# One shared rotation of five PSUM banks in place of three plus two, and 36 stores moved to another engine's DMA queue

## Chip, cores and metric

The kernel runs on one core of a Trainium2 chip. The metric is the device time of one execution in microseconds (us). Most executions of one kernel agree within about 0.4%.

Ratios in this text are the mean time of one kernel's fast runs over that of the other's from the same rounds, with a 95% interval. They are therefore not exactly the ratio of the medians that stand beside them.

Short names: TensorE is PE, VectorE is DVE, ScalarE is ACT, GpSimd is POOL, SyncE is SP in profile lines.

## The reference

The kernel computes the forward pass and all gradients of one layer that adds three terms: the input, a gated feed-forward part ("FFN"), and a state-space convolution ("S4").

```python
xn  = layernorm(x)                                   # 2048 x 576, bf16
gate, up = xn @ W_gate, xn @ W_up                    # 2048 x 4608
ffn = ((gate * (gate > 0)) * up) @ W_down
dt  = exp(log_dt); logdA = dt * (A_re + 1j*A_im)     # 576 x 128
K   = einsum("dn,dnl,dn->dl", C, exp(logdA * l), dt*B).real
out = x + irfft(rfft(xn) * rfft(K)) + xn*Dskip + ffn
# the outputs: out and the gradients of x, A, B, C, log_dt, Dskip, W_gate, W_up, W_down
```

## The kernel before

The FFN part is matmul-bound. It goes through F = 4608 in 12 chunks of 384, and each chunk through the 2048 rows in four groups. The S4 part is a second program, a Python generator, whose instructions are interleaved with FFN's in time. The framework that builds the kernel may order the instructions of each engine anew from their dependencies, so a change of pools or queues can change the instruction order as well.

Each matmul result lies in a PSUM bank until ScalarE or VectorE has copied it out. There are three pools of such banks:

```python
g.psum_mm = pool("psum_mm", 3, space=PSUM)   # FFN matmuls
g.psum_s4 = pool("psum_s4", 3, space=PSUM)   # everything of S4
g.psum_t  = pool("psum_t",  2, space=PSUM)   # FFN transposes
```

The parts of FFN that the argument touches (cuts are marked):

```python
def a_unit(self, c, sg, ft, turns=()):               # first layer: gate, up, dh
    for i, rhs in enumerate((xT, xT, gT)):
        ps = g.psum_mm.tile([P, 512], F32, name="ps_mm")
        for k in range(NK):                           # L235: 5 matmuls of 512 columns
            nc.tensor.matmul(ps[:], lhsT=w[:, k, fs], rhs=rhs[:, k, :], ...)
        ...                                           # one transposition group between two of them
    nc.scalar.activation(rg[:], ps_g[:], ACT.Relu)                     # frees the bank of gate
    nc.vector.scalar_tensor_tensor(upm[:], rg[:], 0.0, ps_u[:], ...)   # frees the bank of up
    nc.vector.tensor_tensor(hT[:], rg[:], upm[:], op=ALU.mult)
    ...                                               # dhb copy frees the third; dgT, duT

def t_steps(self, units):                             # L264: transposes of hT, dgT, duT
    pt = g.psum_t.tile([P, 8, P], BF16, name="pt")
    ...
    g.bal.copy(dst[...], pt[:, 0:JS, :], 512, fp32=False)

def outdx(self, c, sg, j, ...):                       # L291: four output tiles of 288 columns
    ps = g.psum_mm.tile([P, 512], F32, name="ps_mm")
    ...                                               # 3 or 6 matmuls from hT, dgT, duT
    g.bal.copy(o[:, which, hs], ps[:, :DH], DH)       # the osx copy, mostly on ScalarE
```

The part of S4 whose stores move: 36 tiles of exponentials of 128x640 floats (320 KB) are made by VectorE and ScalarE, stored to memory, and read back much later.

```python
exp_ = self.pool(c, "par_ex", 5)                      # five exs buffers
def ex_step(i):
    ex = exp_.tile(shp, F32, name="exs")
    v.tensor_tensor(ex[:], pw[...], self.ev[...], op=ALU.mult)     # L568, VectorE
    nc.scalar.activation(ex[:], ex[:], ACT.Exp)                    # L569, ScalarE
    nc.sync.dma_start(self.ex_dram[:, i], ex[:])                   # L570
```

Of the kernel before, what the change touches and what calls it, by code (L numbers as in the profile page):

```python
# [9 lines left out]
BF16 = mybir.dt.bfloat16  # L10
F32 = mybir.dt.float32
# [3 lines left out]
P = 128  # L15
MAGIC = 12582912.0
TWO_PI = 2.0 * math.pi
PSUM = bass.MemoryType.PSUM
# [52 lines left out]
def dchunks():  # L71
    return [(k, k * P, min(P, D - k * P)) for k in range(NK)]
# [42 lines left out]
def ln_group(g, pools, sg, x4, gT):  # L115
    nc, bal = g.nc, g.bal
    sb, small = pools
    t0 = sg * JS
    mv = small.tile([P, JS, nc.vector.BN_AGGR_DIM], F32, name="mv")
    for j in range(JS):  # L120
        stats = small.tile([P, 2, nc.vector.BN_STATS_DIM], F32, name="stats")
        for s in range(2):
            nc.vector.bn_stats(out=stats[:, s, :], in_=x4[:, j, s * DH:(s + 1) * DH])
        nc.vector.bn_aggr(out=mv[:, j, :], in_=stats[:])
    mvb = small.tile([P, JS, 2], BF16, name="mvb")
    nc.vector.tensor_copy(mvb[:], mv[:])
    veb = small.tile([P, JS], BF16, name="veb")
    nc.vector.tensor_scalar(veb[:], mvb[:, :, 1], 1e-5, None, op0=ALU.add)
    sdb = small.tile([P, JS], BF16, name="sdb")
    nc.scalar.activation(sdb[:], veb[:], ACT.Sqrt)  # L130
    neg = small.tile([P, JS], F32, name="neg")
    nc.vector.tensor_scalar(neg[:], mvb[:, :, 0], -1.0, None, op0=ALU.mult)
    sdf = small.tile([P, JS], F32, name="sdf")
    nc.vector.tensor_copy(sdf[:], sdb[:])
    nc.vector.reciprocal(g.rinv[:, t0:t0 + JS], sdf[:])
    xn4 = sb.tile([P, JS, DP], BF16, name="xn4")
    nc.gpsimd.memset(xn4[:, :, D:DP], 0.0)
    xT = g.xtp.tile([P, NK, JS * P], BF16, name="xT")
    for j in range(JS):
        if j % 2 == 0:  # L140
            nc.vector.tensor_scalar(x4[:, j, :], x4[:, j, :], neg[:, j:j + 1], None, op0=ALU.add)
        else:
            nc.scalar.activation(x4[:, j, :], x4[:, j, :], ACT.Identity, bias=neg[:, j:j + 1])
    for j in range(JS):
        nc.vector.tensor_scalar(xn4[:, j, 0:D], x4[:, j, :], g.rinv[:, t0 + j:t0 + j + 1], None, op0=ALU.mult)
        pt = g.psum_t.tile([P, 8, P], BF16, name="pt")
        for k in range(NK):
            nc.tensor.transpose(out=pt[:, k, :], in_=xn4[:, j, k * P:(k + 1) * P], identity=g.ident_bf[:])
        (nc.vector.tensor_copy if j % 2 == 0 else nc.scalar.copy)(xT[:, :, j * P:(j + 1) * P], pt[:, 0:NK, :])  # L149
    nc.sync.dma_start(g.xT_dram[sg], xT[:])  # L150
    nc.sync.dma_start(g.xn_dram[:, t0:t0 + JS, :], xn4[:, :, 0:D])
    for k, d0, dsz in dchunks():
        nc.sync.dma_start(g.xs_dram[k][:, t0:t0 + JS, :], xn4[:, :, d0:d0 + dsz])
    bal.add(d=6.5, a=2.5)
    return xT, gT

class Ffn:
# [100 lines left out]
    def t_steps(self, units):  # L258
        g, nc = self.g, self.g.nc
        for c, sg, ft in units:  # L260
            for src, dst in zip(self.T[(c, sg, ft)], (self.hN, self.dgN, self.duN)):
                pt = g.psum_t.tile([P, 8, P], BF16, name="pt")
                for j in range(JS):
                    nc.tensor.transpose(out=pt[:, j, :], in_=src[:, j * P:(j + 1) * P], identity=g.ident_bf[:])  # L264
                g.bal.copy(dst[:, sg * JS:(sg + 1) * JS, ft * P:(ft + 1) * P], pt[:, 0:JS, :], 512, fp32=False)
                yield
# [194 lines left out]
class S4:  # L461
# [14 lines left out]
    def pool(self, ctx, name, bufs, side="left"):  # L476
        return ctx.enter_context(self.g.tc.tile_pool(name=name, bufs=bufs, side=side, reuse_waits="tile"))
# [68 lines left out]
    def params(self, pw):  # L546
        g, nc, bal = self.g, self.g.nc, self.g.bal
        v = nc.vector
        with ExitStack() as c:
            pool = self.pool(c, "par_raw", 1)  # L550
            exp_ = self.pool(c, "par_ex", 5)
            raw = pool.tile([P, 6, D], BF16, name="raw")
            nc.sync.dma_start(raw[:], self.par_in[:])
            ldt = pool.tile([P, D], BF16, name="ldt")
            nc.sync.dma_start(ldt[:], self.log_dt.rearrange("(o d) -> o d", o=1).to_broadcast([P, D]))
            yield 1.0
            dt = pool.tile([P, D], F32, name="dtf")
            nc.scalar.activation(dt[:], ldt[:], ACT.Exp)
            nc.sync.dma_start(self.dt_dram[:], dt[:])
            Ar, Ai, Br, Bi, Cr, Ci = (raw[:, i, :] for i in range(6))  # L560
            v.tensor_tensor(pw[:, 0, :], Ar, dt[:], op=ALU.mult)
            bal.add(d=0.7, a=0.7)
            yield 1.0

            def ex_step(i):
                shp = [P, SX, NE]
                ex = exp_.tile(shp, F32, name="exs")
                v.tensor_tensor(ex[:], pw[:, 0, i * SX:(i + 1) * SX].unsqueeze(2).to_broadcast(shp), self.ev[:].unsqueeze(1).to_broadcast(shp), op=ALU.mult)  # L568
                nc.scalar.activation(ex[:], ex[:], ACT.Exp)  # L569
                nc.sync.dma_start(self.ex_dram[:, i], ex[:])  # L570
                bal.add(d=0.75, a=0.65)

            for i in range(0, 8):
                ex_step(i)
                yield 1.0
            p1 = pool.tile([P, D], F32, name="p1")
            p2 = pool.tile([P, D], F32, name="p2")
            v.scalar_tensor_tensor(pw[:, 1, :], Ai, 1.0 / TWO_PI, dt[:], op0=ALU.mult, op1=ALU.mult)
            for j, (y1, y2, op) in enumerate(((Br, Bi, ALU.subtract), (Bi, Br, ALU.add))):
                v.tensor_tensor(p1[:], Cr, y1, op=ALU.mult)  # L580
                v.tensor_tensor(p2[:], Ci, y2, op=ALU.mult)
                v.tensor_tensor(p1[:], p1[:], p2[:], op=op)
                v.tensor_tensor(pw[:, 2 + j, :], p1[:], dt[:], op=ALU.mult)
                bal.add(d=2.6)
                yield 2.0
            for i in range(8, D // SX):
                ex_step(i)
                yield 1.0
# [489 lines left out]
def kernel(  # L1078
# [25 lines left out]
    nc = tc.nc  # L1104
    rows = lambda ap: ap.flatten_outer_dims().rearrange("(p t) d -> p t d", p=P)
    g = G()
# [2 lines left out]
    g.out_dskip = out_9  # L1109
    pool = lambda name, bufs, **kw: ctx.enter_context(tc.tile_pool(name=name, bufs=bufs, **kw))  # L1110
    g.consts = pool("consts", 1)
    g.psum_mm = pool("psum_mm", 3, space=PSUM)
    g.psum_s4 = pool("psum_s4", 3, space=PSUM)
    g.psum_t = pool("psum_t", 2, space=PSUM)
    g.dram = pool("dram", 1, space=DRAM)
    make_consts(g)
    d = lambda name, shape, dt=BF16: g.dram.tile(shape, dt, name=name)
# [14 lines left out]
    def ln(sg, *args):  # L1132
        r = ln_group(g, ln_pools, sg, *args)
        done[0] += 1
        if done[0] == NSG:
            lnctx.close()
        return r
# [79 lines left out]
```

## Time and profile before

| | before |
|---|---|
| median time | 1816.37 us (6 runs, 1814.77 to 1818.72) |
| TensorE busy | 96% |
| VectorE, ScalarE busy | 75%, 65% |
| sum of TensorE's idle gaps | 72.7 us |

The page of the kernel before, its first two parts and lines of its fifth and sixth. The last line, of the sixth part, ends with the median time from issuing a transfer to the signal that it is complete; this text calls that landing. A group's line gives the instruction, its count, its busy time and mean duration, and after the second bar the idle time of its engine just before it and what ended most of it:

```profile
PE 1736.5 (96%) x16449; PEld 1185.3 (65%) x16449; DVE 1359.2 (75%) x3181; ACT 1185.5 (65%) x2710; POOL 205.4 (11%) x246
...
DMA  8788999678568566776857856856665577994873
...
L67 ACT CAST osx<-ps_mm 128x288 bf16<-128x288 f32 x675 | 261.9, 426 | 70.3 <-PE ps_mm L291 67.1
...
L291 PE MATMUL ps_mm<-wf,dgT 128*128 128x288 bf16 x1152 | 207.3, 287 | 12.8 <-ACT osx L67 6.5
...
ex_dram<-exs SPq DMA_DIRECT2D x36, 320.0 KB, 3.8
```

TensorE is the limit. The second group waits before it starts, and what it waits for is the osx copy. That copy only reads a bank; the matmuls do not read its result. So this is a wait for a free bank. The waits of TensorE in the kernel before (us in total, times, longest):

```profile
PE ps_mm L204 <- DMA gT<-in_gT_dram: 8.9, 1, 8.9
PE ps_mm L291 <- DVE upm L245: 8.1, 12, 1.1
PE ps_mm L291 <- ACT osx L67: 6.5, 10, 1.8
PE ps_mm L235 <- ACT obd L67: 4.7, 2, 4.5
...
PE ps_mm L291 <- DVE hT L247: 3.8, 3, 1.9
PE ps_mm L291 <- ACT dhb L67: 3.5, 8, 1.0
```

Matmuls overlap, so short waits vanish inside "busy". A finer count takes the interval between successive matmul starts, less the usual interval after a matmul of that shape, and books the excess on whatever released the later matmul.

For the stores, the timeline of the kernel before from 121 to 147 us, with cuts (start, duration, engine, line, what; in brackets the idle time before and its releaser):

```profile
121.38 0.82 ACT L569 ACTIVATE exs<-exs 128x640 f32<-128x640 f32 x1
...
137.66 1.84 SPq L570 DMA_DIRECT2D ex_dram<-exs  x1
...
144.02 0.83 DVE L568 TENSOR_TENSOR exs<-pw,ev 128x640 f32<-128x640 f32 x1 [7.24 <-DMA ex_dram<-exs]
...
144.88 0.74 ACT L569 ACTIVATE exs<-exs 128x640 f32<-128x640 f32 x1 [7.74 <-DVE exs L568]
...
145.53 0.50 ACT L67 CAST obd<-ps_mm 128x432 bf16<-128x432 f32 x1
...
146.08 1.44 PE L235 MATMUL ps_mm<-gT,wd_160 128*128 128x512 bf16 x3 [4.46 <-ACT obd L67]
```

SyncE issued a store at 137.66 whose exponential was finished before. VectorE stood still 7.24 us for a buffer of exponentials, ScalarE 7.74 us behind it, and TensorE 4.46 us for the obd copy that stands behind the next exponential on ScalarE.

### The profile page before, as it was taken

What the parts mean: (1) busy time and instruction counts of PE and PEld (TensorE: products, weight loads), DVE (VectorE), ACT (ScalarE), POOL (GpSimd) and SP (SyncE); (2) the same over time, 40 slices, a digit from 0 to 9 for tenths busy, and PEclk for the clock granted to TensorE, in tenths of its full rate; (3) what the DMA queues carried; (4) which work ended last, traced back from release to release, by engine and by line L of the source; (5) the groups of instructions that cost most, each with busy time, mean ns of one, the idle gap of its engine ahead of it and who ended that gap; (6) DMA issues with size and microseconds to landing.
All of it is one profiled execution on the core that took longest, in us unless ns stands there. A gap on an engine that the chain in (4) does not pass through costs nothing. (4 is left out here: it accounts for less than half of the span.)

```text
span 1813.8 us, 42303 instructions
## 1 busy us (share of the span) xinstructions
PE 1736.5 (96%) x16449; PEld 1185.3 (65%) x16449; DVE 1359.2 (75%) x3181; ACT 1185.5 (65%) x2710; POOL 205.4 (11%) x246
## 2 busy tenths in 40 slices
PE   7998998999999999999999999999999999999998
PEld 5664556667566666766756766766676675676776
DVE  7575886676888789678787899989979863983551
ACT  5874874686578487568468658748746845764551
POOL 0200012012022011011102101101111100110000
PEclk9999999999999999999999999999999999999999
DMA  8788999678568566776857856856665577994873
GB/s 292 262 309 309 319 257 286 192 185 244 163 134 207 176 178 148 222 187 146 224 156 187 226 164 145 219 173 151 167 179 146 91 220 244 269 292 153 268 245 96
DMA packets 239004, 373.30 MB, mean 206 GB/s; under 512 B 49490, under 2 KB 153428, under 8 KB 237268
## 3 DMA queue, kind: packets, MB, share of 16 engines
q1 hardware_dynamic: 212836, 304.09, 51.4%
q0 software_dynamic: 24384, 51.92, 18.3%
q10 hardware_dynamic: 1584, 14.60, 2.3%
q8 instruction: 128, 2.10, 0.5%
q14 instruction: 72, 0.59, 0.1%
HBM read 233.10 MB, written 137.43 MB: 204 GB/s over the span
## 5 line engine op out<-in xcount | busy, mean ns | idle before, releaser
L67 ACT CAST osx<-ps_mm 128x288 bf16<-128x288 f32 x675 | 261.9, 426 | 70.3 <-PE ps_mm L291 67.1
L304 POOL DMA_DIRECT2D acc_dram<-osx x160 | 138.8, 868 | 1066.9 <-ACT osx L67 716.3
L291 PE MATMUL ps_mm<-wf,dgT 128*128 128x288 bf16 x1152 | 207.3, 287 | 12.8 <-ACT osx L67 6.5
L344 PEld LDWEIGHTS <-rows 128*128 128x128 bf16 x1536 | 146.2, 98 | 96.6 <-issue 6.9
L291 PE MATMUL ps_mm<-wf,duT 128*128 128x288 bf16 x1152 | 206.0, 287 | 0.0
L291 PE MATMUL ps_mm<-wf,hT 128*128 128x288 bf16 x1152 | 185.5, 288 | 13.4 <-DVE upm L245 6.8
L235 PE MATMUL ps_mm<-gT,wd_160 128*128 128x512 bf16 x705 | 178.0, 381 | 5.9 <-ACT obd L67 4.7
L235 PE MATMUL ps_mm<-xT,wd_158 128*128 128x512 bf16 x720 | 181.0, 379 | 0.8 <-ACT xT L149 0.5
L235 PE MATMUL ps_mm<-xT,wd_159 128*128 128x512 bf16 x720 | 179.9, 379 | 0.0
L245 DVE SCALAR_TENSOR_TENSOR upm<-rg,ps_mm 128x512 bf16<-128x512 bf16 x144 | 98.2, 682 | 92.2 <-PE ps_mm L235 70.4
L328 PE MATMUL ps_mm<-rows,hN 128*128 128x144 bf16 x2304 | 158.4, 226 | 0.0
L328 PEld LDWEIGHTS <-hN 128*128 128x128 bf16 x2304 | 147.4, 98 | 4.1 <-issue 1.4
L67 ACT CAST obw<-ps_mm 128x384 bf16<-128x384 f32 x104 | 49.6, 478 | 147.7 <-PE ps_mm L344 116.4
L344 PE MATMUL ps_mm<-dgN,rows 128*128 128x384 bf16 x768 | 137.7, 329 | 0.6 <-ACT rg L243 0.6
L291 PEld LDWEIGHTS <-dgT 128*128 128x128 bf16 x1152 | 107.3, 98 | 45.9 <-issue 20.7
L344 PE MATMUL ps_mm<-duN,rows 128*128 128x384 bf16 x768 | 136.6, 326 | 0.3 <-DVE upm L245 0.3
L291 PEld LDWEIGHTS <-hT 128*128 128x128 bf16 x1152 | 105.0, 98 | 43.2 <-issue 13.7
L291 PEld LDWEIGHTS <-duT 128*128 128x128 bf16 x1152 | 112.8, 98 | 29.2
L243 ACT ACTIVATE rg<-ps_mm 128x512 bf16<-128x512 f32 x144 | 87.1, 605 | 54.5 <-PE ps_mm L235 53.0
L903 DVE TENSOR_REDUCE Sm<-pr 128x8 f32<-128x256 f32 x288 | 118.9, 413 | 3.6
L67 ACT CAST dhb<-ps_mm 128x512 bf16<-128x512 f32 x141 | 83.9, 595 | 56.6 <-PE ps_mm L235 54.5
L235 PEld LDWEIGHTS <-wd_159 128*128 128x128 bf16 x720 | 65.3, 98 | 61.8 <-issue 1.5
(2517 smaller groups left out, 3523.5 us busy)
## 6 DMA issues: line engine op xcount, KB each, us to landing
acc_dram<-osx POOLq DMA_DIRECT2D x176, 288.0 KB, 4.7
gT<-in_gT_dram SPq DMA_DIRECT2D x48, 640.0 KB, 6.1
xT<-xT_dram SPq DMA_DIRECT2D x44, 640.0 KB, 5.7
rows<-in_gq_dram SPq DMA_DIRECT2D x48, 576.0 KB, 4.3
wf<-in_Wf_dram ACTq DMA_DIRECT2D x11, 1296.0 KB, 9.2
ex_dram<-exs SPq DMA_DIRECT2D x36, 320.0 KB, 3.8
ex<-ex_dram SPq DMA_DIRECT2D x36, 320.0 KB, 4.0
out_dram<-obw SPq DMA_DIRECT2D x96, 96.0 KB, 2.5
```

Source lines behind the costliest of these rows:

```text
L67: self.nc.scalar.copy(out, in_)
L235: nc.tensor.matmul(ps[:], lhsT=w[:, k, fs], rhs=rhs[:, k, :], start=(k == 0), stop=(k == NK - 1))
L243: nc.scalar.activation(rg[:], ps_g[:], ACT.Relu)
L245: nc.vector.scalar_tensor_tensor(upm[:], rg[:], 0.0, ps_u[:], op0=ALU.is_gt, op1=ALU.mult)
L291: nc.tensor.matmul(ps[:, cs], lhsT=lt, rhs=rh, start=(i == 0), stop=(i == len(mms) - 1))
L304: nc.gpsimd.dma_start(g.acc_dram[:, t, :, :], o[:], accum_op=ALU.add)
L328: nc.tensor.matmul(ps[:, ft * 144:(ft + 1) * 144], lhsT=self.hN[:, st, ft * P:(ft + 1) * P], rhs=gq[:, st, :], start=(st == 0), stop=(st = ...
L344: nc.tensor.matmul(ps[:, :Fc], lhsT=xs[:, st, 0:P], rhs=src[:, st, :], start=(st == 0), stop=(st == ST - 1))
L903: nc.vector.tensor_reduce(out=Sm[:, vi, s0 + dd:s0 + dd + DG, :], in_=pr[:], op=ALU.add, axis=AX.X)
```

## The change

It has two intents. FFN's matmuls and transposes take their banks from one rotation of five (banks handed out in a fixed turn), so that neither waits while the other has a bank to spare. And the stores leave SyncE's queue, where they stood behind other transfers.

```diff
-        pt = g.psum_t.tile([P, 8, P], BF16, name="pt")
+        pt = g.psum_mm.tile([P, 512], F32, name="ps_mm")[:].bitcast(BF16).rearrange("p (k t) -> p k t", t=P)
   (the same at both places that transpose: layer norm and t_steps)
-                nc.sync.dma_start(self.ex_dram[:, i], ex[:])
+                nc.scalar.dma_start(self.ex_dram[:, i], ex[:])
-    g.psum_mm = pool("psum_mm", 3, space=PSUM)
+    g.psum_mm = pool("psum_mm", 5, space=PSUM)
     g.psum_s4 = pool("psum_s4", 3, space=PSUM)
-    g.psum_t = pool("psum_t", 2, space=PSUM)
```

More of the change, by code (lines that the diff above doesn't have):

```diff
@@ L261, in t_steps @@
             for src, dst in zip(self.T[(c, sg, ft)], (self.hN, self.dgN, self.duN)):
-                pt = g.psum_t.tile([P, 8, P], BF16, name="pt")
+                pt = g.psum_mm.tile([P, 512], F32, name="ps_mm")[:].bitcast(BF16).rearrange("p (k t) -> p k t", t=P)
                 for j in range(JS):
```

## The prediction

> **What bounds the kernel.** TensorE. The page's first part shows it busy 1736.5 of 1813.8 us (96%), VectorE 75%, ScalarE 65%. Summing TensorE's idle gaps over the trace gives 72.7 us. Matmuls overlap, so I also took intervals between successive matmul starts, less the usual interval for that shape (122 ns for 288 columns): this shows waits hidden in "busy".
>
> **Where the two PSUM pools cost time.** By what released them, these excesses at the ps_mm writers are: output-gradient matmuls (L291) waiting for the osx copy 14 us (74 times), for upm 11 us (20), for the dhb copy 6 us (16), for rg 2 us and the VectorE osx copy 1.6 us; first-layer matmuls (L235) waiting for obd 5 us (2). These are waits for a bank in a rotation of three: about 40 us (2.2% of the span). Transposes (L264) waiting for one of their two buffers cost some 5 us. Waits for data, loads and the S4 part's own banks stay. The waits are short (0.1 to 1 us): ScalarE needs about 0.43 us to empty each 288-column tile and falls behind in bursts. The page "PSUM — Partial Sum Buffer" of the Trainium skill gives eight banks: 3+3+2 before and 5+3 after, so only the sharing changes.
>
> **What sharing does.** In the stretches of output matmuls without transposes, TensorE can run five tiles ahead instead of three: nearly all of the 34 us at L291 is eligible. Against it, a unit that alternates three matmul groups with three transposes reuses a bank after five allocations, about 2.5 matmul groups instead of three, and a late copy of a transpose now holds up matmuls too. Laying a five-deep rotation over the recorded times, I count about 130 old waits that vanish and about 30 new ones, some of several us. Estimate: 15 to 20 us gained, 5 to 8 given back.
>
> **What the store change does.** 36 stores, all between 101 and 213 us. On SyncE's queue they stand in line behind other transfers that wait: an exponential finished at about 129 us was stored only at 137.7, VectorE then waited 7.2 us for an exs buffer (144.0), ScalarE 7.7 us, and TensorE 4.5 us (146.1, for obd). In all VectorE waits 13.5 us for these stores. Issued by ScalarE right after the exponential this goes away: about 5 us. Cost: the issues took a median of 0.44 us on SyncE's queue, 0.33 on ScalarE's (its wf loads), so 36 x 0.35 = 13 us of ScalarE's sequencer in a stretch of 115 us where ScalarE is busy 76.7 us; TensorE feels perhaps 2 to 3 us. No bandwidth is gained: the skill's "DMA: Bandwidth & Descriptors" (Issuing engines are not separate DMA queues) says all issuers share the same 16 engines; DMA share is 0.94 there.
>
> **Prediction.** About -14 us: 1802 us, range 1788 to 1818. Faster by over 2%: 0.05; within: 0.92; slower: 0.03.
>
> **Signs.** Right: L291's waits for osx, upm and dhb fall from 40 us to below 15; transposes and L235 wait a little more; VectorE's wait for ex_dram vanishes, so does the 4.5 us wait near 146 us; SyncE issues 36 fewer. TensorE's busy time stays near 1736 (matmuls are the same), its gaps fall to about 60 us.
>
> **What would make it wrong.** ScalarE may be behind on average in those stretches, not only in bursts: then deeper buffers only move the wait. A changed instruction order may shift S4 work by more than either effect.

## The result and the profile after

The changed kernel takes 1817.69 us (median of 10 runs, 1814.03 to 1826.24), the kernel before 1817.88 us (20 runs). The ratio is 1.0004, interval 0.9992 to 1.0016: no change. The predicted gain of 14 us did not come.

The page of the changed kernel, the lines that answer to those above:

```profile
PE 1727.2 (95%) x16449; PEld 1185.4 (65%) x16449; DVE 1358.5 (75%) x3181; ACT 1183.3 (65%) x2710; POOL 205.3 (11%) x246
...
DMA  8789889578567665867757856856665478994873
...
L67 ACT CAST osx<-ps_mm 128x288 bf16<-128x288 f32 x675 | 255.4, 428 | 62.6 <-PE ps_mm L291 59.1
...
L291 PE MATMUL ps_mm<-wf,dgT 128*128 128x288 bf16 x1152 | 207.2, 288 | 4.6 <-DVE upm L245 2.0
...
ex_dram<-exs ACTq DMA_DIRECT2D x36, 320.0 KB, 5.4
```

The L291 group's idle time fell from 12.8 to 4.6 us and the osx copy is no longer what ended it. That half did what it was meant to do. But the stores now take 5.4 us to land in place of 3.8. The waits of TensorE:

```profile
PE ps_mm L291 <- DVE hT L247: 12.5, 5, 7.2
PE ps_mm L204 <- DMA gT<-in_gT_dram: 9.3, 1, 9.3
PE ps_mm L291 <- DVE upm L245: 6.6, 7, 2.9
PE ps_s_1748 L609 <- DVE fA_1669 L61: 2.7, 1, 2.7
PE ps_s_2492 L624 <- ACT s_ug L67: 2.4, 1, 2.4
```

New at the top stands a wait for hT, which is data and not a bank, with one wait of 7.2 us; below it stand waits of S4's matmuls (ps_s). Here is what VectorE waited for at the exs multiplies between 95 and 235 us, before and then after:

```profile
DVE exs L568 <- DMA ex_dram<-exs: 13.5, 5, 7.2
```

```profile
DVE exs L568 <- DMA ex_dram<-exs: 25.9, 13, 3.8
```

The wait that should have vanished has doubled.

Where in the run the time goes shows when the same instruction is found in both traces. The lag of the relu copies (144 in each trace) behind those of the kernel before, in us, by their time in the kernel before; a minus sign is a lead:

```
time in before             80    146    218    400    752   1429    end
changed kernel           -0.2   +3.0   +7.6   +7.7   +4.9   +0.9   -0.4
banks alone (below)      -0.6   -1.8   -2.7   +1.0   -1.8   -5.6   -5.1
stores alone (below)     +0.3   +5.9  +10.0  +10.7  +10.9  +12.2  +12.9
4 + 4 banks (below)      -1.5   -2.9   -6.6   -4.7  -10.2  -14.8  -12.7
```

The changed kernel loses 7.6 us between 80 and 218 us, which is where nearly all of the 36 stores are (103 to 233 us), and has won it back by the end. So "no change" looks like a sum of two effects, and the first question for the chip was whether it is a sum of the two halves of the change. The ends in the last column are those of one profiled execution of each kernel, the times further down those of all runs: the profiled execution of the stores-alone kernel was its slowest (1828.45 us against a median of 1824.32).

The timeline of the changed kernel shows the largest single loss:

```profile
103.42 0.96 ACTq L570 DMA_DIRECT2D ex_dram<-exs  x2
103.52 0.43 SPq L182 DMA_DIRECT2D wd_156<-in_Wd_dram  x1
...
105.70 0.67 DVE L245 SCALAR_TENSOR_TENSOR upm<-rg,ps_mm 128x512 bf16<-128x512 bf16 x1
...
106.93 0.33 SPq L196 DMA_DIRECT2D xT<-xT_dram  x1
...
110.12 0.83 DVE L568 TENSOR_TENSOR exs<-pw,ev 128x640 f32<-128x640 f32 x1 [3.75 <-DMA ex_dram<-exs]
111.81 0.83 DVE L568 TENSOR_TENSOR exs<-pw,ev 128x640 f32<-128x640 f32 x1 [0.86 <-ACT exs L569]
112.55 0.42 DVE L247 TENSOR_TENSOR hT<-rg,upm 128x512 bf16<-128x512 bf16 x1
...
113.03 0.42 PE L291 MATMUL ps_mm<-wf,hT 128*128 128x288 bf16 x1 [7.24 <-DVE hT L247]
```

And VectorE in the kernel before at the same place:

```profile
106.55 0.82 DVE L568 TENSOR_TENSOR exs<-pw,ev 128x640 f32<-128x640 f32 x1 [0.59 <-ACT fA_1702 L67]
107.29 0.68 DVE L245 SCALAR_TENSOR_TENSOR upm<-rg,ps_mm 128x512 bf16<-128x512 bf16 x1
107.89 0.82 DVE L568 TENSOR_TENSOR exs<-pw,ev 128x640 f32<-128x640 f32 x1
108.62 0.42 DVE L247 TENSOR_TENSOR hT<-rg,upm 128x512 bf16<-128x512 bf16 x1
```

Read it from the end. TensorE waits for hT. The multiply that makes hT stands in VectorE's stream behind two exs multiplies. The first of them needs a free exs buffer, and all five hold exponentials whose stores have not landed. The first store was issued at 103.42 and landed at 110.03, 6.6 us later. In the kernel before, the first store was issued at 103.2 and landed at 106.5, 3.3 us later, and hT was ready four microseconds sooner.

Why did it land later, although it was issued at the same time? Before, SyncE issued the stores first and the large weight loads after them, from 110.4 us on. With the stores gone from its queue, SyncE ran ahead and issued the loads of wd and xT from 103.06 on. In the trace of single DMA packets, the first packet of the first store starts at 107.22, 3.8 us after its issue; before, it started 1.4 us after (104.55). The transfer then shares the DMA engines: between 110 and 112 us the stores' queue moved 206 GB/s and SyncE's queue 200. The first stores are the extreme: over all 36, counted by their packets, the median from issue to first packet is 2.0 us before and 2.7 after, and to the end of the last packet 3.1 and 4.6. (The landing times on the page are medians of the 27 and 26 stores whose completion could be told.)

The Trainium skill says as much: "DMA: Bandwidth & Descriptors", section "Issuing engines are not separate DMA queues", states that transfers issued by the scalar, sync or gpsimd engine all run on the same 16 DMA engines and interleave. The section "Queues, rings and completion order" adds that the two queues have no descriptor generator of their own and that each DMA engine takes turns between them. The equal rates agree with the turns. That the late first packet is due to a shared descriptor generator fits the page but was not isolated by a run.

### The profile page after: what moved, and what is told of

Its sections match the earlier page's. It is cut to its first block, busy times and chain, and to the rows that moved or that the text cites. A ratio compares the mean times of both kernels' runs of the same rounds, so it can differ in the third digit from the quotient of the medians.

```text
span 1813.4 us, 42318 instructions
## 1 busy us (share of the span) xinstructions
PE 1727.2 (95%) x16449; PEld 1185.4 (65%) x16449; DVE 1358.5 (75%) x3181; ACT 1183.3 (65%) x2710; POOL 205.3 (11%) x246
## 5 line engine op out<-in xcount | busy, mean ns | idle before, releaser
L67 ACT CAST osx<-ps_mm 128x288 bf16<-128x288 f32 x675 | 255.4, 428 | 62.6 <-PE ps_mm L291 59.1
L291 PE MATMUL ps_mm<-wf,dgT 128*128 128x288 bf16 x1152 | 207.2, 288 | 4.6 <-DVE upm L245 2.0
L291 PE MATMUL ps_mm<-wf,duT 128*128 128x288 bf16 x1152 | 207.0, 288 | 0.0
L291 PE MATMUL ps_mm<-wf,hT 128*128 128x288 bf16 x1152 | 182.4, 287 | 19.1 <-DVE hT L247 12.5
L235 PE MATMUL ps_mm<-xT,wd_155 128*128 128x512 bf16 x720 | 180.2, 379 | 4.0 <-ACT xT L149 1.6
L235 PE MATMUL ps_mm<-xT,wd_156 128*128 128x512 bf16 x720 | 180.2, 379 | 0.0
L235 PE MATMUL ps_mm<-gT,wd_157 128*128 128x512 bf16 x705 | 178.1, 380 | 1.1 <-DMA gT<-in_gT_dram 1.1
L291 PEld LDWEIGHTS <-hT 128*128 128x128 bf16 x1152 | 104.1, 98 | 50.4 <-DVE hT L247 16.7
L291 PEld LDWEIGHTS <-duT 128*128 128x128 bf16 x1152 | 113.0, 98 | 30.9 <-issue 1.3
L291 PEld LDWEIGHTS <-dgT 128*128 128x128 bf16 x1152 | 107.9, 98 | 32.4 <-issue 7.3
L235 PEld LDWEIGHTS <-wd_155 128*128 128x128 bf16 x720 | 66.2, 98 | 64.3 <-issue 6.2
```

The source lines that it names most:

```text
L67: self.nc.scalar.copy(out, in_)
L291: nc.tensor.matmul(ps[:, cs], lhsT=lt, rhs=rh, start=(i == 0), stop=(i == len(mms) - 1))
```

## The experiments

For the bank accounts below, this is the finer count of the section on the profile before, in us, from one profile of each kernel. "S4" are the waits of S4's matmuls for ScalarE or VectorE, banks and data together; "hT" are L291's waits for hT, dgT or duT. The traces of the experiments e1 to e12 lack about 146 of the 16449 matmul records, so differences of 2 or 3 us mean nothing.

```
                           FFN banks   S4    hT     median time
before                       50.8     33.3   4.5    1817.88
changed kernel               25.2     48.5  13.4    1817.69
banks alone      (5, 3)      23.0     56.3   5.9    1808.28
stores alone     (3+2, 3)    55.3     31.9  11.4    1824.32
four, four       (4, 4)      47.4     30.8   4.5    1802.76
four, three      (4, 3)      42.9     44.1   4.3    1811.96
three, five      (3, 5)      89.4     15.0   1.4    1827.96
four, four, 8 exs            42.7     29.4   4.5    1797.05
```

The brackets name the banks of FFN and of S4.

A part of the time stands in none of these waits. In every profile the granted TensorE clock is 1.0 except for stretches of 3.4 us or a multiple of it in which it is 0.5. A 288-column matmul that starts in such a stretch is followed by the next after a median of 240 ns in place of 122. These longer intervals, less the usual ones (and without those over 2.3 times the usual, which hold a wait), add up to 10.4 us in the kernel before, 9.6 in the changed kernel, 8.5 with the banks alone, 9.5 with the stores alone, 5.7 with four and four banks, and 17.5 with the stores on GpSimd's queue, whose profiled span is 23 us longer than that of the banks alone. So the clock does not explain the result of the change, but it is a part of the difference between some of the runs below.

### The two halves apart

Two theories. A: sharing the banks gains, moving the stores costs, and the two cancel. B: sharing gains nothing, because a wait removed from one bank comes back as another wait, and the lag at 218 us is an accident of instruction order.

**e1_banks_only**, the changed kernel with the stores put back:

```diff
-                nc.scalar.dma_start(self.ex_dram[:, i], ex[:])
+                nc.sync.dma_start(self.ex_dram[:, i], ex[:])
```

> Five shared banks alone; the stores stay on SyncE's queue. Theory A (the two halves of the change cancel: sharing gains, moving the stores costs): about 7 us faster than before, some 1810 us; the exs stretch (100 to 215 us) runs as in the kernel before. Rival B (sharing gains nothing, since the engines that empty the banks are the limit and a removed bank wait comes back as another wait; the 5 us lag and its later recovery are accidents of instruction order): within 2 us of before, about 1817.

Measured: 1808.28 us against 1818.9 us, ratio 0.9944 (0.9931 to 0.9957). VectorE's wait for exs buffers is 8.8 us and the lag at 218 us is gone (-2.7). Theory A holds here.

**e2_stores_only**, the kernel before with the same line changed the other way:

> Stores on ScalarE's queue alone; banks 3+3+2 as before. Theory A: about 6 to 7 us slower than before, some 1824 us, VectorE's idle time before the exs multiplies for the stores up from 13.5 us to about 25 us, lost between 100 and 235 us and not recovered later. Rival B: within 2 us of before; the lag at 230 us is absent or is recovered.

Measured: 1824.32 us, ratio 1.0033 (1.0019 to 1.0047). VectorE waits 27.7 us for exs buffers. The loss of 10 us stands at 218 us and is not won back later. Theory B falls: each half has its effect alone, with the sign that A gave it. On top of the shared banks the stores cost 1.0004 / 0.9944 = 1.0060. That this is more than alone is barely clear of the noise: each of the three ratios has an interval of about 0.0013 to either side.

### How the stores cost

ScalarE's waits in the stores-only run between 95 and 235 us show something that the prediction did not have:

```profile
ACT exs L569 <- DMA b_ug<-A_ug: 3.9, 1, 3.9
ACT obw L67 <- DMA rows<-xs_dram: 3.8, 1, 3.8
...
ACT obd L67 <- DMA A_ug<-fA: 2.8, 1, 2.8
```

ScalarE needs none of these transfers; SyncE issued them. In the program built from the changed kernel, 32 of the 36 stores on ScalarE wait for two things, their exponential and one of eight DMA semaphores (counters that signal completion) that all the transfers of both queues use in turn. Three instructions of ScalarE there, without those that only wait:

```
199 L570 DMACopy ex_dram<-exs 128x640 [waits DMAHW7_49,Activation_49]
200 L67 TensorCopy obd<-ps_mm 128x3x144 [waits PE_49]
201 L570 DMACopy ex_dram<-exs 128x640 [waits DMAHW1_49,Activation_49]
```

The wait stands in ScalarE's own stream, and the copies behind it wait too: 12.2 us of idle ScalarE that a transfer ended in the changed kernel, 18.8 us in the stores-only run, against none in the kernel before. All but 1.7 and 2.7 us of it was for transfers that ScalarE has no use for. The Trainium skill's "DMA: Bandwidth & Descriptors", section "Anatomy of one DMA", which describes transfers issued by GpSimd, says that DMA engines do not wait on semaphores and that such a wait happens on the issuing sequencer; the idle times of ScalarE here agree with it. So there were two candidates: (1) late landing, which makes VectorE stand before hT, and (2) ScalarE's own stream, by its issues and these foreign waits.

**e3_both_exs8**, the changed kernel with more buffers:

```diff
-            exp_ = self.pool(c, "par_ex", 5)
+            exp_ = self.pool(c, "par_ex", 8)
```

> The whole change, with eight exs buffers in place of five, so that VectorE has no store to wait for so soon. If the stores on ScalarE's queue cost time because they land late (5.4 us) and VectorE and ScalarE stand still for a free exs buffer: the wait falls from 25.9 us to under 8 us, and the kernel gains 5 to 7 us, to about 1811. If they cost time because each issue occupies ScalarE's instruction stream (0.33 us x 36): the wait falls as well, but the time stays within 2 us of the changed kernel, about 1817.

Measured: 1814.56 us, ratio 0.9975 (0.9959 to 0.9991). That is 0.3% better than the changed kernel, as (1) expected. At the place shown above, hT is done at 108.6 us in place of 113.0, and the 7.2 us wait is 2.1 us. But VectorE's wait fell only from 25.9 to 20.6 us, not below 8: the build used the new buffers to place multiplies earlier, and they wait again. The number was missed and the cause was only half shown.

**e5_banks_exs8**, the control: the same edit on the banks-only kernel.

> Five shared banks, stores on SyncE's queue, eight exs buffers in place of five: the control for the two store runs with eight buffers. In the banks-only run VectorE waits only 8.8 us for exs buffers, so if buffers matter through that wait alone, there is little to gain: within 3 us of the banks-only run, 0.992 to 0.995 of before.

Measured: 1807.22 us, ratio 0.9940 (0.9928 to 0.9953), the same as with five buffers. VectorE's wait was 17.8 us, twice that of the banks-only run, at the same time. So the length of VectorE's wait alone does not tell the cost; it depends on what stands behind it. With eight buffers, ScalarE's queue costs 0.9975 / 0.9940 = 1.0035, with five 1.0060; the difference of the two is within their noise.

**e9_stores_gpsimd**, the banks-only kernel with `nc.gpsimd.dma_start` for the stores:

> Five shared banks, and the stores issued by GpSimd, which has little to do between 100 and 215 us. In the store runs ScalarE stood still 12 to 19 us in that stretch until transfers of SyncE's queue had landed, which no ScalarE data needs. If that standing still is what the stores on ScalarE's queue cost: here ScalarE has no such waits (under 4 us) and the time is that of the banks-only run or up to 4 us better, 0.992 to 0.995 of before. If the cost is that stores land late once they are off SyncE's queue, so that VectorE waits for an exs buffer: VectorE's wait stays above 20 us, and the time is near the changed kernel's, 0.998 to 1.001.

Measured: 1830.02 us, ratio 1.0061 (1.0042 to 1.0080). ScalarE's foreign waits are gone (0.3 us), and yet it is the slowest run, slower than either branch expected. VectorE waits 27.3 us; the stores land a median of 6.0 us after their issue. TensorE's waits between 95 and 240 us:

```profile
PE ps_s L609 <- DVE fA L61: 10.6, 2, 7.9
PE ps_s L624 <- DVE s_ug L61: 4.8, 1, 4.8
PE ps_mm L291 <- DVE hT L247: 4.2, 1, 4.2
```

All three are waits for VectorE. ScalarE's standing still is therefore not needed for a loss; late landing goes with one in its absence. That landing alone makes it is not shown: some 30 of VectorE's 3181 instructions stand at other places than in the banks-only run, and half-clock stretches took 9 us more.

**e10_gpsimd_exs8**, the same with eight buffers:

> As the run with stores on GpSimd's queue (1.006 of before, VectorE waiting 27.3 us for exs buffers, no ScalarE waits for foreign transfers), with eight exs buffers. If the cost of taking the stores off SyncE's queue is that they share the DMA engines with the large loads that SyncE now issues at once, land later (6 us) and keep VectorE waiting for buffers: VectorE's wait falls by 10 us or more and the time by 8 us or more, to 1.002 or below. If the cost is something else about the issuing engine: the time stays within 3 us of 1.006.

Measured: 1820.60 us, ratio 1.0009 (0.9996 to 1.0022), about 9 us better; VectorE's wait fell from 27.3 to 12.4 us. As (1) expected. It remains 0.7% above the control with SyncE's queue, so three more buffers are not the whole answer.

**e12_half_stores**, the changed kernel with stores of half the size (the result is wrong; the gradients of A, B and C are off by up to 10%):

```diff
-                nc.scalar.dma_start(self.ex_dram[:, i], ex[:])
+                nc.scalar.dma_start(self.ex_dram[:, i, 0:SX // 2], ex[:, 0:SX // 2])
   (and the load in load_ex reads that half twice)
```

> The changed kernel, but each of the 36 stores on ScalarE's queue writes only the first half of its tile (160 KB in place of 320), and the later load reads that half twice. The result is wrong on purpose. The number of issues and their cost on ScalarE are unchanged. If late landing is what costs: landing falls from 5.4 us to under 4.5 us, VectorE's wait from 25.9 us to under 15 us, and the time to 0.996 of before or less. If the issues on ScalarE are what costs: the time stays at 0.998 to 1.001. (Less DMA traffic in a stretch where the engines are over 0.9 busy may help by itself, so a gain alone would not part the two; the wait of VectorE must fall with it.)

Measured: 1812.88 us, ratio 0.9969 (0.9955 to 0.9984); landing 4.7 us, VectorE's wait 19.9 us. The direction is that of (1), but all three numbers were missed, the wait of VectorE by the most. The stores were half as large and still landed late: the first was issued at 101.9 us and landed at 107.4, its first packet 3.3 us after the issue. What stands before a store counts more than its own size.

**e13_quarter_act** and **e14_quarter_sp**: a quarter of each store, on ScalarE's and on SyncE's queue. **e15_half_sp**: half, on SyncE's queue, beside the half-size run above. All have five shared banks. Their outputs are wrong, which doesn't matter for the times.

> Five shared banks, stores on ScalarE's queue, each cut to a quarter of its tile (80 KB; wrong on purpose, the later load repeats the quarter). To be read beside the same cut with the stores on SyncE's queue. With full stores the queue of ScalarE costs 0.6% of the time (1.0004 against 0.9944). If that is late landing through contention with the large loads: with a quarter of the bytes the two runs lie within 0.15% of each other. If it is ScalarE's own stream (0.33 us per issue, and standing still until transfers of SyncE's queue have landed): the difference stays at 0.3 to 0.6%.

> The control for the quarter stores: on SyncE's queue. 0.990 to 0.994 of before (less traffic in the stretch where the DMA engines are over 0.9 busy).

> The control for the half stores (0.9969 of before on ScalarE's queue): half stores on SyncE's queue. If landing is what ScalarE's queue costs, the difference shrinks with the bytes: this run at 0.993 to 0.995, a difference of 0.2 to 0.4% between the 0.6% of full stores and that of quarter stores. If ScalarE's stream is what costs, the difference is that of full stores, 0.991 here.

Measured: quarter on ScalarE 1812.54 us, ratio 0.9971 (0.9954 to 0.9987); quarter on SyncE 1817.75 us, 0.9999 (0.9982 to 1.0016); half on SyncE 1819.25 us, 1.0003 (0.9982 to 1.0025).

No theory expected this. Less traffic made SyncE's version slower by 0.55% and ScalarE's faster by 0.33%, so the order of the two is reversed. The traces say what happened to the controls: in the quarter run on SyncE's queue VectorE now stands 8.04 us at one exs multiply, from 124.70 to 132.74 us, and TensorE 7.3 us at 134.7 for the copy behind it. The build had put that multiply earlier; in the banks-only run VectorE waited there from 132.33 us, for 3.46 us. The quarter run on SyncE's queue, with cuts:

```profile
121.88 0.38 ACTq L185 DMA_DIRECT2D wf<-in_Wf_dram  x1
...
123.95 1.12 SPq L570 DMA_DIRECT2D ex_dram<-exs  x2
...
132.74 1.56 DVE L568 TENSOR_TENSOR exs<-pw,ev 128x640 f32<-128x640 f32 x2 [8.04 <-DMA ex_dram<-exs]
...
134.72 0.40 PE L609 MATMUL ps_s<-sig,Sx 128*128 128x288 bf16 x1 [7.26 <-DVE fA L61]
```

VectorE waited for a store of only 80 KB on SyncE's own queue. It was issued at 123.95 us and landed at 132.65, 8.7 us later: the packets of a load of 1296 KB that ScalarE had issued (wf) ran from 124.2 to 130.6 us, and the first packet of the store from 129.7. In the banks-only run the same store was issued at 132.01, after that load. So a store landed late on SyncE's queue too, where it met a large load. Its size counted for little: the half and the quarter run of each queue have the same order of instructions on VectorE, ScalarE, GpSimd and SyncE, and the same time: 0.9969 and 0.9971 on ScalarE's queue, 1.0003 and 0.9999 on SyncE's. Of the 10.6 us between the profiled spans of the two quarter runs, 6.4 are half-clock stretches (15.3 against 8.9 us).

Between the queues, and against the full stores, these controls did not hold the instruction order fixed, and the order is worth as much as the effect. So they do not settle theory (2): a fixed price of the issues and foreign waits on ScalarE is neither shown nor excluded.

What the runs show about the stores, then: off SyncE's queue full stores cost 0.3 to 0.6% from ScalarE and 1.2% from GpSimd (1.0061 / 0.9944); in each of these runs TensorE waits for VectorE, and VectorE for a late store, at one or two places of 4 to 8 us; a store on SyncE's queue that met a large load did the same; more buffers take part of it away. How the rest divides between landing, instruction order and ScalarE's foreign waits stays open: no kernel was built that moves the full stores and keeps the order.

### Where the gain of the banks went

In the changed kernel FFN's bank waits fell by 25.6 us (50.8 to 25.2), and S4's waits rose by 15.2 us (33.3 to 48.5). Either S4's three banks became the short ones, or ScalarE and VectorE are behind and any wait only moves.

**e4_four_four**, stores on SyncE's queue:

```diff
-    g.psum_mm = pool("psum_mm", 5, space=PSUM)
-    g.psum_s4 = pool("psum_s4", 3, space=PSUM)
+    g.psum_mm = pool("psum_mm", 4, space=PSUM)
+    g.psum_s4 = pool("psum_s4", 4, space=PSUM)
```

> Stores on SyncE's queue; the eight banks split into four shared by the FFN part and four for the S4 part (five and three in the first run of this set). In the changed kernel the FFN part's bank waits fell by about 26 us, but the S4 part's waits rose from 33 to 48 us. If that is because S4's three banks became the short ones: S4's waits fall to about 35 us or less, FFN's rise by less than 10 us, and the time beats the banks-only run by 3 us or more. If the engines that empty banks are simply behind in bursts, an extra bank on either side only moves the wait: same time as the banks-only run within 3 us, or slower.

Measured: 1802.76 us, ratio 0.9908 (0.9893 to 0.9922), 6 us better than five and three. S4's waits fell to 30.8 us. FFN's rose by 24 us, more than expected, to near where they were before the change, and still the kernel is faster. So the count of waits is a guide to where a bank is short and not a sum that equals the time.

**e6_four_three**, four shared banks, three for S4, one bank unused:

> Four shared banks for the FFN part, three for S4, one bank left unused; stores on SyncE's queue. It parts the 4+4 run (0.991 of before) into its two moves. If the FFN part has no use for a fifth bank: within 2 us of the 5+3 run, 0.994 of before, and the 4+4 run's further 6 us came from S4's fourth bank alone. If the fifth bank carries part of the gain: 0.996 to 1.000 of before, and S4's fourth bank is worth 10 us or more.

Measured: 1811.96 us, ratio 0.9972 (0.9955 to 0.9989). This takes the steps apart. Sharing four banks beats three plus two, with one bank fewer: 0.28%. FFN's fifth bank is worth another 0.28% (0.9972 to 0.9944). The same bank given to S4 is worth 0.64% (0.9972 to 0.9908), as the second branch expected. Each of these steps is uncertain by about 0.2%, and each split is a new build with its own instruction order; that S4's waits fall step by step with its banks (56.3, 30.8, 15.0 us with three, four, five banks, all eight in use) speaks for the banks.

**e8_three_five**, the same two lines with 3 and 5:

> Three shared banks for the FFN part, five for S4; stores on SyncE's queue. If S4's banks are the short ones throughout, it is as good as 4+4 or better (0.991 or less). If the split has to be balanced, FFN's bank waits come back (over 60 us in place of some 47 in 4+4) and the time is at or above the kernel before.

Measured: 1827.96 us, ratio 1.0049 (1.0034 to 1.0064). S4's waits fell to 15.0 us and FFN's rose to 89.4. The split has to be balanced.

**e7_all_eight**, one rotation of eight for FFN and S4:

```diff
-    g.psum_mm = pool("psum_mm", 5, space=PSUM)
-    g.psum_s4 = pool("psum_s4", 3, space=PSUM)
+    g.psum_mm = pool("psum_mm", 8, space=PSUM)
+    g.psum_s4 = g.psum_mm
   (and one tile name for both)
```

> One rotation of all eight banks for both parts; stores on SyncE's queue. If a shared rotation is good because no part waits while another has a free bank: at least as good as 4+4, 0.989 or less. If a rotation is harmed by its slowest reader, since a late copy of one part then holds up the other part too: worse than 4+4 by 3 us or more, and the matmuls of the FFN part are seen waiting for S4's readers.

Measured: 1806.37 us, ratio 0.9933 (0.9915 to 0.9951): better than before, and by the medians about 4 us worse than four and four, though the two intervals overlap. Its runs lie from 1801.01 to 1810.02 us and the profiled one is the fastest, 1.8 us faster than that of four and four, so the profile cannot show the 4 us. It shows one large loss early in the run. Its longest wait of TensorE:

```profile
PE ps_mm L539 <- ACT d_o L447: 14.9, 3, 10.2
```

L539 is S4's first transposition, which waited for its data for 10.2 us at 71.8 us; the lag at 80 us is 17.4 us, and at the end the kernel leads by 14.5 us. That the FFN part is held up by S4's readers was not what its profile showed. That the order of the early instructions was the harm is a guess that no run tested.

### The best version

**e11_four_four_exs8**: four and four, stores on SyncE's queue, eight exs buffers.

> Four shared banks for FFN, four for S4, stores on SyncE's queue, eight exs buffers: the candidate to beat both kernels. The 4+4 run gave 0.991 of before, its VectorE waited 14 us for exs buffers. If those waits still cost TensorE there: 0.987 to 0.990. If not: 0.990 to 0.992.

Measured: 1797.05 us (4 runs, 1795.50 to 1800.63), ratio 0.9882 (0.9869 to 0.9895), correct. It is 1.2% faster than both kernels. VectorE's wait is 10.8 us. In five and three, eight buffers gave nothing; here they gave 0.26% (uncertain by about 0.2%), and why they do so only here was not studied.

## Why the prediction was wrong

- **"About -14 us: 1802 us".** Measured: ratio 1.0004. Two terms were summed, and one of them had the wrong sign.
- **Banks: "15 to 20 us gained, 5 to 8 given back".** The net was right, 7 to 15 us predicted and 0.56%, about 10 us, measured alone. But it was right partly by luck: both terms were too small. 25.6 us of FFN's bank waits went (L291's waits for osx, upm, dhb and rg from 34.6 to 11.6 us, as the signs said), and 15.2 us came back. It did not come back where the prediction looked, at transposes and L235, but at S4's three banks, which the prediction had put among the things that "stay".
- **Stores: "Issued by ScalarE right after the exponential this goes away: about 5 us".** This step failed. It took the wait at 137 us in the kernel before for a matter of queue position alone, although that store, once issued, still took 6.3 us to land. The mean time from the end of an exponential to the issue of its store did fall, from 5.8 to 1.8 us, and the wait for obd at 146 us did vanish. But landing went from 3.8 to 5.4 us, VectorE's wait from 13.5 to 25.9 us, and a new wait of 7.2 us appeared at 113 us. Measured cost: 0.33% alone, 0.60% on top of the banks, in place of a gain of 2 to 3 us.
- **"No bandwidth is gained"** was right (313 GB/s before and 321 after, between 100 and 215 us), and the prediction did not draw the conclusion: SyncE, freed of the stores, starts other transfers sooner, and these meet the stores on the same engines.
- **"13 us of ScalarE's sequencer"** was about right (36 issues took 12.0 us); what share of the loss it is was not isolated. The waits of ScalarE for transfers, 12.2 us and nearly all of them foreign, were not foreseen.
- **"SyncE issues 36 fewer"**: right. **"TensorE's busy time stays near 1736, its gaps fall to about 60 us"**: wrong, 1727.2 and 81.5 us; short waits hidden between overlapping matmuls became fewer and longer.
- The chance of 0.92 for "within 2%" was well placed, and the range held the result; the forecast of a change was wrong.

## What to carry to other kernels

When one consumer of PSUM gets more banks, look at the consumer next to it: here the same bank was worth more to the part that was not being looked at (0.64% against 0.28%, each uncertain by about 0.2%), and an even split of shared pools beat the uneven one. Before a transfer is moved to another engine's queue, ask what the freed queue will start at that moment, what the new issuer has to wait for in its own stream, and which engine's stream stands behind the buffer that the transfer frees. Test the halves of a double change apart: a time that does not move can be two effects of 0.6% with opposite signs.

## What the Trainium skill lacked or had wrong

- "DMA: Bandwidth & Descriptors", section "Issuing engines are not separate DMA queues", says that issuing from several engines only saves the time to initiate the transfer. It lacks the other direction: in the changed kernel the first of the stores moved to ScalarE's queue had its first packet 3.8 us after its issue in place of 1.4 us, and the stores landed in a median of 5.4 us in place of 3.8; with the stores alone moved (5.5 us) the kernel was 0.33% slower.
- The same page says that a semaphore wait happens on the issuing sequencer. It lacks the size of what this can do to a computing engine: ScalarE stood idle 12.2 and 18.8 us for transfers, nearly all of them issued by another engine, where the build gives the transfers of both queues eight semaphores in turn.
- "DMA: Bandwidth & Descriptors", table "Issuing engine by pattern", names SyncE for simple stores. The runs agree, for full stores: SyncE 0.9944, ScalarE 1.0004, GpSimd 1.0061 of the kernel before, with the same banks. With quarter stores the first two were reversed (0.9999 and 0.9971), in another instruction order.
- "PSUM — Partial Sum Buffer" gives the number of banks and asks for prompt evacuation. It has nothing on dividing them between two interleaved programs: 3+2 and 3, 5 and 3, 4 and 4, 3 and 5 banks gave 1, 0.9944, 0.9908 and 1.0049.
